# A state-space layer's kernel tables from the distinct bf16 times alone, in a tuned four-layer kernel

## The chip, the cores and the metric

The kernel runs on one core of a Trainium2 chip. Its engines each work through an instruction queue of their own: PE (TensorE: matmuls; PEld is its weight loading), DVE (VectorE), ACT (ScalarE), POOL (GpSimd), and SP (SyncE), whose queue issues most DMAs. An instruction that has to wait for another engine waits at the head of its queue, and everything behind it waits too. The metric is the device time of one execution in microseconds (us), as a median of runs. The order of the instructions on each queue is fixed when the kernel is built.

## The reference

Two kinds of layer, each used twice on `x` of 2048 positions by 512 channels, each with a layer norm ahead of it and a residual behind it. The A layer is a state-space convolution; the B layer is attention over a window of 8 positions, 2 apart, with 32 heads of 16.

```python
l = arange(L).astype(bfloat16)            # L = 2048
P = exp(logdA[:, :, None] * l[None, None, :])     # D = 512, N = 128
K = einsum("dn,dnl,dn->dl", Cc, P, dB).real
y = irfft(rfft(pad(K)) * rfft(pad(u)))[:L] + u * Dskip
...
x = x + A(layernorm(x)); x = x + B(layernorm(x))
x = x + A(layernorm(x)); x = x + B(layernorm(x))
```

The times `l` are rounded to bf16. bf16 keeps 8 bits of a number, so only 641 different times are left of 2048: every one up to 256, then every 2nd, 4th and 8th. The kernel `K` is therefore piecewise constant beyond 256.

## The kernel before

There are five planned parts: preparation, kernel tables with the first convolution, the first B layer (B1), the second A layer (A2, which reuses the spectrum of `K` from DRAM) and the second B layer (B2). "Stage 1" below is the first two parts. In each part, `Plan.op` collects operations; the order in which they are issued is a list of numbers written out in `ORDERS`, one string for each part, and with it each engine's queue is fixed. `pl.either` names two ways for one piece of work (a copy on ACT or on DVE, a transposition by DMA or by PE), and the list takes one.

**Preparation** (`prepare`). From the parameters it forms the pole's step `exp(dt A)`, its repeated squares (the ladder `lad`, L630/L634), and from each of them the multipliers that the tables need, in bf16, in an A and a B form, so that a complex product is two elementwise products and one sum with the halves of the second exchanged (`multipliers`, L579). It normalizes the first input `X` (L196 on DVE, L692 on ACT), and it makes the tables of unit 0 and most of unit 1.

**Tables** (`Tables`). A unit `hc` is 64 channels; there are 8. The kernel at lag `32 i + e` is a product of a power from an X table (`e`, 32 of them) and one from a Y table (64 of them). For each unit, DVE doubles the number of powers level by level: `level` (L406/L411 for the A product, L412 for the B product), `level_sum` (L419) for the sum; `high` and `high_sum` (L426, L427, L432) for the upper half of the X table; `y_product` (L475) for the Y tables. Some of the sums are done by two identity matmuls on PE into PSUM (`sum_mm`, L450 and L451) and an ACT copy back (L455). The tile `Ttab` has two buffers, so the next unit's tables may be built while PE still reads the last one's. Channels lie in pairs (`t`) with real and imaginary part (`c`) and the power (`e`) in the order `h c e t`.

**Contraction** (`contract`, L488 and L491): 256 small matmuls for each unit sum over the 128 states and give K for 64 channels in PSUM (`psk`). It is copied to `KTq`, stored to `k_scratch` in DRAM (L839 is the line of `store`), and fetched from there in the arrangement that the FFT wants (`KT`, L846). The last 64 channels don't take the trip; they go by `spread_rows` and other matmuls (`last`).

**The convolution.** An FFT of length 4096 in two steps. The first (`spectrum`, L862 `ps_s`) multiplies by constant matrices `F1`; ACT copies the result to `Z` (L867), which is transposed by DMA or by PE (`pt`) into `zt`; the second step multiplies by `C2` (`xp`), and ACT copies to `sp_u` or `sp_k`. `u_fft` does that for the input and `k_fft` for `K`, for each group `dc` of 128 channels. DVE then multiplies the spectra (L952, `pa`) and in some places joins the four partial products to two (L957, L958; elsewhere PE does the joining, with more matmuls into `vp`). The inverse gives `vp`, `VT` (L979), `ps_y` (L999) and adds into `X` (L1003). All PSUM results of this part but `psk` share three buffers, `psA`, each of which comes free when ACT or DVE has copied it out. DVE's and ACT's queues are in order, PE's too.

## Time and profile before

| what | us |
|---|---|
| median of 3 runs (lowest, highest) | 467.45 (466.55, 467.87) |
| span of the profiled execution | 468.0 |
| DVE busy, share of the span | 440.1, 94% |
| PE busy | 396.0, 85% |
| ACT busy | 347.7, 74% |
| first work of B1 on DVE (end of stage 1) | 199.56 |
| mean granted clock of TensorE | 0.991 |

The page gives, for each group of instructions, line, engine, operation and tiles, then the count, the busy time in us, the mean duration of one in ns, and the idle time of the engine just before them with what ended it. A duration runs from an instruction's start to its end; back-to-back instructions overlap a little, so the distance from one start to the next is the better price of one. Windows give each engine's busy time, with the number of instructions, in a stretch of the span. In timelines a row is start, duration, instruction, and in square brackets the idle time before it and its releaser.

The 40-slice view shows the shape:

```profile
PE   2520866879799999899999989979999999999996
DVE  6999999999999998699999999989996899999995
ACT  6999857897788898666796357999996667763452
```

Each slice is 11.7 us. The first 17 of them are stage 1.

### The profile page before, as it was taken

What the parts mean: (1) busy time and instruction counts of PE and PEld (TensorE: products, weight loads), DVE (VectorE), ACT (ScalarE), POOL (GpSimd) and SP (SyncE); (2) the same over time, 40 slices, a digit from 0 to 9 for tenths busy, and PEclk for the clock granted to TensorE, in tenths of its full rate; (3) what the DMA queues carried; (4) which work ended last, traced back from release to release, by engine and by line L of the source; (5) the groups of instructions that cost most, each with busy time, mean ns of one, the idle gap of its engine ahead of it and who ended that gap; (6) DMA issues with size and microseconds to landing.
All of it is one profiled execution on the core that took longest, in us unless ns stands there. A gap on an engine that the chain in (4) does not pass through costs nothing. (4 is left out here: it accounts for less than half of the span.)

```text
span 468.0 us, 12380 instructions
## 1 busy us (share of the span) xinstructions
PE 396.0 (85%) x5248; PEld 243.6 (52%) x5248; DVE 440.1 (94%) x595; ACT 347.7 (74%) x543; POOL 21.2 (5%) x90
## 2 busy tenths in 40 slices
PE   2520866879799999899999989979999999999996
PEld 1310543535576667643576444666776445563453
DVE  6999999999999998699999999989996899999995
ACT  6999857897788898666796357999996667763452
POOL 1000000000000001300000000000000010100210
PEclk9999999999999999999999989989999999999999
DMA  8992263047596684640113131389957200213584
GB/s 234 187 287 92 14 148 92 11 83 147 130 205 114 137 173 142 122 69 1 63 46 89 46 67 23 62 254 169 161 107 109 57 22 14 79 46 78 60 157 123
DMA packets 111419, 49.36 MB, mean 105 GB/s; under 512 B 88811, under 2 KB 104572, under 8 KB 111108
## 3 DMA queue, kind: packets, MB, share of 16 engines
q1 hardware_dynamic: 109924, 47.70, 47.5%
q0 software_dynamic: 1152, 0.61, 1.0%
q8 instruction: 41, 0.67, 0.6%
q10 hardware_dynamic: 288, 0.26, 0.2%
q14 instruction: 14, 0.11, 0.1%
HBM read 15.88 MB, written 8.13 MB: 51 GB/s over the span
## 5 line engine op out<-in xcount | busy, mean ns | idle before, releaser
L1755 DVE TENSOR_TENSOR prod<-VX,L 128x512 bf16<-128x512 bf16 (+2 forms) x72 | 75.2, 1101 | 0.7 <-PE po L1771 0.3
L1579 DVE TENSOR_TENSOR prod<-qT,kT 128x4096 bf16<-128x4096 bf16 (+1 forms) x40 | 72.3, 1857 | 1.6 <-ACT qT L1504 1.5
L1771 PE MATMUL po<-prod,sb_ident 128*128 128x512 bf16 x224 | 52.0, 379 | 2.1 <-DVE prod L1755 1.1
L1771 PEld LDWEIGHTS <-sb_ident 128*128 128x128 bf16 x224 | 21.7, 98 | 27.7 <-issue 2.3
L450 PE MATMUL ps_sum<-Ttab,sb_ident 128*128 128x512 bf16 x36 | 14.7, 408 | 22.0 <-DVE Ttab L411 21.2
L1855 PE MATMUL ps_o<-wo_t,oT 128*128 128x512 bf16 x128 | 32.3, 379 | 0.0
L1534 PE MATMUL ps_v<-wv,U 128*128 128x256 bf16 x256 | 31.3, 272 | 1.0 <-ACT L L1718 0.3
L867 ACT CAST Z<-ps_s 128x1024 bf16<-128x1024 f32 (+1 forms) x32 | 29.3, 986 | 2.5 <-PE ps_s L862 1.8
L1480 PE MATMUL ps_qk<-U,wqk 128*128 128x512 bf16 x128 | 29.7, 379 | 0.2 <-ACT qT L1485 0.2
L1545 ACT ACTIVATE VX<-ps_v,rs 128x256 bf16<-128x256 f32 x64 | 26.5, 471 | 4.5 <-PE ps_v L1534 4.1
L1534 PEld LDWEIGHTS <-U 128*128 128x128 bf16 x256 | 24.4, 98 | 8.9 <-issue 4.3
L1499 PE MATMUL ps_qk<-U,wqk 128*128 128x512 bf16 x128 | 29.0, 379 | 0.0
L475 DVE TENSOR_TENSOR Ttab<-Ttab,MPA 128x2048 bf16<-128x2048 bf16 (+2 forms) x20 | 28.4, 1431 | 0.1
L1789 ACT CAST ot<-po 128x1024 bf16<-128x1024 f32 x14 | 13.9, 1013 | 18.2 <-PE po L1771 18.2
L475 DVE TENSOR_TENSOR Y2tab<-Ttab,MPB 128x6144 bf16<-128x6144 bf16 (+1 forms) x13 | 27.2, 2119 | 0.0
L488 PE MATMUL psk<-Ttab 128*32 128x64 bf16 x1024 | 20.7, 197 | 6.1 <-issue 3.2
L488 PEld LDWEIGHTS <-Ttab 128*32 128x32 bf16 x1024 | 18.1, 95 | 10.9 <-issue 9.5
L455 ACT CAST Ttab<-ps_sum 128x1024 bf16<-128x1024 f32 (+1 forms) x22 | 18.2, 873 | 7.0 <-PE ps_sum L451 6.8
L1590 PE MATMUL Lp<-prod,sb_bones 128*32 128x512 bf16 x256 | 21.0, 411 | 1.9 <-DVE prod L1579 1.7
L412 DVE TENSOR_TENSOR Ttab<-Ttab,MUB 128x256 bf16<-128x256 bf16 (+4 forms) x36 | 22.3, 621 | 0.0
L491 PE MATMUL psk<-Y2tab,Ttab 128*32 128x48 bf16 x1024 | 20.3, 190 | 1.9 <-issue 1.3
L952 DVE TENSOR_TENSOR pa<-sp_u,sp_k 128x2048 bf16<-128x2048 bf16 x16 | 19.3, 1220 | 2.2 <-ACT X L1003 1.0
(255 smaller groups left out, 1020.1 us busy)
## 6 DMA issues: line engine op xcount, KB each, us to landing
kt_scratch<-sp_k SPq DMA_DIRECT2D x16, 256.0 KB, 2.9
Kt<-kt_scratch SPq DMA_DIRECT2D x16, 256.0 KB, 5.5
X<-in_A_u_dram SPq DMA_DIRECT2D x8, 256.0 KB, 5.3
X<-in_A_u_dram SPq DMA_DIRECT2D x4, 512.0 KB, 6.0
out_dram<-X SPq DMA_DIRECT2D x16, 128.0 KB, 2.4
k_scratch<-KTq SPq DMA_DIRECT2D x7, 256.0 KB, 2.4
KT<-k_scratch SPq DMA_DIRECT2D x7, 256.0 KB, 3.8
VX<-VX SPq DMA_DIRECT2D x4, 448.0 KB, 3.7
```

What stands on the lines that cost most here:

```text
L412: nc.vector.tensor_tensor(self.spare(hc, False)[:, x0:x1, :, :, 0:m, :].rearrange("n x h c e t -> n (x h c) e t"), src, mult(1), ALU.mult)
L475: nc.vector.tensor_tensor(d, src.to_broadcast([128, c, n, 2 * EYB]), mm, ALU.mult)
L488: nc.tensor.matmul(o.rearrange("e (s i) -> e s i", s=2), xs, T[:, 1:3, h, m // 2, :, t], start=(m == 0), stop=False, skip_group_check=True)
L867: nc.scalar.copy(box["Z", kind, dc][:, 0:n // 8, :, jq * 32:(jq + 1) * 32].rearrange("p g r k -> p r g k"), box.pop(("s1", kind, dc, jq))[ ...
L1480: nc.tensor.matmul(ps[:], wqk[:, ct, f0:f0 + 128], XT[:, ct // 2, 4 * s:4 * s + 4, ct % 2, :], start=(ct == 0), stop=(ct == 3))
L1499: nc.tensor.matmul(box[name][:, k * 512:k * 512 + 512], wqk[:, ct, f0:f0 + 128], XT[:, ct // 2, 4 * s:4 * s + 4, ct % 2, :], start=(ct == ...
L1534: nc.tensor.matmul(ps[:, jj].rearrange("p t h d -> p (t h d)"), XT[:, ct // 2, j + jj, ct % 2, :], wv[:, ct, fp * 256:(fp + 1) * 256], sta ...
L1545: nc.scalar.activation(out, ps, ACT.Identity, scale=r)
L1579: nc.vector.tensor_tensor(pr[:], windows(q, 0, 2), windows(kT[fp][:, a:a + n2, col(w):col(w) + 1024], -DIL * 128, 2), ALU.mult)
L1755: nc.vector.tensor_tensor(p2[:].rearrange("p w j t d h -> p w (j t) d h"), windows(v, -DIL * 256, taps), l.to_broadcast([128, taps, nj * 2 ...
L1771: nc.tensor.matmul(po[:, c:c + 512], ident[:], p2[:, t, k + j:k + j + 2].rearrange("p j t d h -> p (j t d h)"), start=first, stop=stop)
L1855: nc.tensor.matmul(ps, oT[:, ft // 2, o:o + 128], wo_t[:, ft, :], start=(ft == 0 and not res), stop=(ft == 3))
```

## The change

The kernel `K` is built only at the lags that bf16 times can take. Every lag is the sum of one of 20 Y lags and one of 32 X lags (multiples of 8), so a unit has 20 + 32 powers in place of 64 + 32. One tile `Ttab` holds them, in the order `h e c t`, and a second tile `Btab` holds the last product of the X table, whose sum is left out: the contraction takes both terms. Neither has a second buffer: a unit uses the half of the tile given by its parity. The tables are built in chunks of one or two units (`CHUNKS`), the first two within the preparation. Each `step` is a product by the A multiplier, one by the B multiplier into a scratch tile, and an add (`add`) which reads the scratch with real and imaginary part exchanged (`[:, :, ::-1]`). The sums by PE and ACT are gone, and so are the multipliers for one more power and for a cube.

The contraction still has 256 matmuls a unit, with 24 columns. Its result is copied to `kq`, 72 small matmuls with a constant (`select`, `sel`) move the rows to where they are wanted (`pk`), and two copies put them in `KT`; the store to and the fetch from DRAM are gone, and `last` with them. As `K` is piecewise constant, the first FFT step of `K` takes 31 constant pairs of matrices `FK` (2 MB, loaded by four DMAs on GpSimd's queue), by which a row of `KT` stands for all times that share it. Lag 0 is a sum of its own (`k0_sum`), added with `Dskip` as a second row of `D2`.

All five orders in `ORDERS` are new; with them 12 pairs of joins are on DVE where 7 were. Two constants (`minus`, `down`) are loaded after stage 1. The diff, cut to its core (the orders, the multipliers' arrangement, removed functions and renamed arguments are left out; line numbers used for the changed kernel are: seed L424, products L456 and L463, add L468, contraction L481, `D2` L704, `FK` L769, first FFT step L825, products of spectra L916):

```diff
+Y_LAGS = (258, 262, 516, 260, 264, 520, 772, 776, 1032, 1288, 1544, 1800, 1, 5, 2, 6, 3, 7, 4, 8)
+NY, NX, NKC = 20, 32, 24
+X_LAGS = tuple(8 * e for e in range(NX))
+TOP = (1032, 1288, 1544, 1800)
+SLOTS = (TOP + (264, 776, 520, 8), TOP + (516, 772, 260, 4), (1, 5, 2, 6, 258, 3, 262, 7))
...
-    def __init__(self, nc, tc, es, M, cb):
-        self.nc, self.M, self.cb = nc, M, cb
-        self.tt = es.enter_context(tc.tile_pool(name="t_t", bufs=2))
-        self.ty = es.enter_context(tc.tile_pool(name="t_y", bufs=1))
-        self.T, self.Y2 = {}, {}
+    def __init__(self, nc, tc, es, M):
+        self.nc, self.M = nc, M
+        pool = es.enter_context(tc.tile_pool(name="t_t", bufs=1))
+        self.scratch = es.enter_context(tc.tile_pool(name="t_s", bufs=2))
+        self.T = pool.tile([128, UNIT, NY + NX, 2, 2], BF, name="Ttab")
+        self.B = pool.tile([128, UNIT, 32, 2, 2], BF, name="Btab")
+        self.cb1 = pool.tile([128, D // 2, 2, 2], BF, name="cb1")
+        self.box = {}
...
+    def seed(self, copy, u, n):
+        h0, p0 = u % 2 * 32, u * 32
+        copy(self.T[:, h0:h0 + 32 * n, self.Y0].rearrange("n h c t -> n h (c t)"),
+             self.cb1[:, p0:p0 + 32 * n].rearrange("n h c t -> n h (c t)"))
+    def views(self, u, n, what):
+        h0, p0, M = u % 2 * 32, u * 32, self.M
+        T = self.T[:, h0:h0 + 32 * n]
+        ps = slice(p0, p0 + 32 * n)
+        if what in (0, 1, 2):
+            m = 4 << what
+            v = T[:, :, self.Y0:self.X0 + 8].rearrange("n h (x e) c t -> n h x (e c t)", x=2)
+            return v[:, :, :, 0:m], v[:, :, :, m:2 * m], [self.spread(x[:, what, ps].rearrange("p h x c t -> p (h x) c t"), 1 << what) for x in M.joint]
+        if what in (3, 4):
+            m = 4 << what
+            v = T[:, :, self.X0:].rearrange("n h e c t -> n h (e c t)")
+            return v[:, :, 0:m], v[:, :, m:2 * m], [self.spread(x[:, what - 3, ps], 1 << what) for x in M.single]
...
+    def times(self, u, n, what):
+        src, dst, (ma, mb) = self.views(u, n, what)
+        nc.vector.tensor_tensor(dst, src, ma, ALU.mult)
+        if what == 4:
+            h0 = u % 2 * 32
+            b = self.B[:, h0:h0 + 32 * n, 16:].rearrange("n h e c t -> n h (e c t)")
         else:
+            t = self.box[u, what] = self.scratch.tile([128, UNIT * 16], BF, name="Tscr", tag="Tscr")
+            b = t[:, 0:self.elements(n, what)]
+        nc.vector.tensor_tensor(b, src, mb, ALU.mult)
+    def add(self, u, n, what):
+        dst = self.views(u, n, what)[1]
+        b = self.box.pop((u, what))[:, 0:self.elements(n, what)].rearrange("n (e c t) -> n e c t", c=2, t=2)[:, :, ::-1]
+        self.nc.vector.tensor_tensor(dst, dst, b, ALU.add)
-    def level_sum(self, hc, lev, x0=0, x1=2):
-        m = 1 << lev
-        d = self.T[hc][:, x0:x1, :, :, m:2 * m, :].rearrange("n x h c e t -> n (x h) c (e t)")
-        b = self.spare(hc, False)[:, x0:x1, :, ::-1, 0:m, :].rearrange("n x h c e t -> n (x h) c (e t)")
-        self.nc.vector.tensor_tensor(d, d, b, ALU.add)
...
+    def contract(self, psk, u, ds0, ds1):
+        nc, T, B = self.nc, self.T, self.B
         for ds in range(ds0, ds1):
             for m in range(4):
                 for g in range(4):
+                    d = g * 16 + ds
+                    h, t, c = u % 2 * 32 + d // 2, d % 2, m % 2
+                    xs = T[:, h, self.X0:, c, t] if m < 2 else B[:, h, :, 1 - c, t]
+                    y = T[:, h, 0:12, c, t]
+                    rhs = bass.AP(y.tensor, y.offset, [list(y.ap[0]), [32, 2], [4, 12]])
+                    nc.tensor.matmul(psk[32 * g:32 * g + 32, ds, :].rearrange("p (z y) -> p z y", z=2), xs, rhs, start=(m == 0), stop=(m == 3),
+                                     skip_group_check=True)
+CHUNKS = ((0, 1), (1, 1), (2, 2), (4, 2), (6, 1), (7, 1))
+EARLY = 2
+def table_ops(pl, nc, T, u, n, seeds, free, casts):
+    e = T.elements
+    o = moved(pl, nc, ("seed", u), 0.15 + 0.1 * n, 0.08 + 0.066 * n, lambda copy: T.seed(copy, u, n), seeds, free)
+    steps, last = {}, []
+    def step(what, *after):
+        steps[what] = []
+        for v, m in ((u, 1), (u + 1, 1)) if n == 2 and what in (2, 3) else ((u, n),):
+            us, key = e(m, what) / 1920 + 0.069, ("sc", v, what)
+            a = pl.op("V", 2 * us, lambda v=v, m=m: T.times(v, m, what), *after, take=[] if what == 4 else key)
+            if what != 4:
+                a = pl.op("V", us, lambda v=v, m=m: T.add(v, m, what), a, drop=key)
+            steps[what].append(a)
+        return steps[what]
+    def cast(*ks):
+        return [casts[k] for k in ks] if casts else []
+    for lev in range(3):
+        o = step(lev, o, cast(*T.JOINT[lev]))
+    step(3, o, cast(6))
+    a = step("a", o, cast(8))
+    b = step("b", o, cast(9))
+    c = step("c", b, cast(8))
+    d = step("d", c, cast(9))
+    return [step(4, steps[3], cast(7)), a, step("e", d, cast(9))]
...
+    def k0_sum():
+        ps = box["k0"] = pst.tile([1, D], F32, name="k0", tag="ptq")
+        nc.tensor.matmul(ps[:], ones[:, 0:1], cb[:, :, 0, :], start=True, stop=True)
+    a = pl.op("P", 0.25, k0_sum, modes[2], pl.outer(("raw", "block")), take=("ptq", "k0"))
+    moved(pl, nc, ("k0",), 0.48, 0.61, lambda copy: copy(D2[0:1, :], box.pop("k0")[:]), a, drop=("ptq", "k0"))
...
+    def start_sum():
+        o = T.cb1[:].rearrange("n p c t -> n p (c t)")
+        nc.vector.tensor_tensor(o, o, box["cbs"][:, :, ::-1], ALU.add)
...
-        pl = Plan(T=2, Y2=1, psk=2, psA=3, Z=1, zt=4, KT=1, kt=4, xc=8, pa=2, VT=1)
+        pl = Plan(psk=2, kq=2, psA=3, Z=1, zt=4, KT=2, kt=4, xc=NXC, pa=2, VT=1, sc=2)
+        def contract(u):
+            def mm(ds):
+                if ds == 0:
+                    box["psk", u] = psK.tile([128, 16, NKC], F32, name="psk", tag="psk")
+                T.contract(box["psk", u], u, ds, ds + 4)
+            def evac(copy):
+                kq = box["kq", u] = kp.tile([128, NKC, 16], BF, name="kq", tag="kq")
+                copy(kq[:].rearrange("p y d -> p d y"), box.pop(("psk", u))[:])
+            def select():
+                kq = box.pop(("kq", u))
+                pk = box["pk", u] = psK.tile([128, 4, 2, 3, 16], F32, name="pk", tag="psk")
...
+            def placed(copy):
+                if u % 2 == 0:
+                    box["KT", u // 2] = kp.tile([128, 3, 2, 128], BF, name="KT", tag="KT")
+                c0 = u % 2 * UNIT
+                pk = box.pop(("pk", u))
+                for e in range(2):
+                    copy(box["KT", u // 2][:, :, e, c0:c0 + UNIT].rearrange("p s (g d) -> p g s d", g=4), pk[:, :, e])
+            p = []
+            for ds in range(0, 16, 4):
+                p = [pl.op("P", 0.54, lambda ds=ds: mm(ds), Td[u], p, take=[] if ds else ("psk", "k", u))]
+            Cd[u] = p
+            a = moved(pl, nc, ("psk", u), 0.4, 0.48, evac, p, take=("kq", u), drop=("psk", "k", u))
+            a = pl.op("P", 0.6, select, a, take=("psk", "sel", u), drop=("kq", u))
+            Kd[u] = moved(pl, nc, ("placed", u), 0.5, 0.55, placed, a, [] if u % 2 == 0 else Kd[u - 1], take=[] if u % 2 else ("KT", u // 2), drop=("psk", "sel", u))
...
+        def k_fft(dc, b0, nb):
+            c0, c1 = b0 * 32, (b0 + nb) * 32
+            def mats(j, r):
+                x = box.get(("KT", dc))
+                todo = [(FK[:, i, r, :], x and x[:, s // 2, s % 2, c0:c1]) for s, i in pairs[j]]
+                if j == 0 and r == 0:
+                    todo.append((C["onesr"][:], D2[:, dc * DCH + c0:dc * DCH + c1]))
+                return todo
+            last = [("KT", dc)] if b0 + nb == 4 else []
+            spectrum("k", dc, b0, nb, mats, lambda jq: [Rd["FK", jq], *[Kd[u] for u in range(dc * 2, dc * 2 + 2) if (u % 2) * 2 < b0 + nb]], last)
+            for c in range(b0, b0 + nb):
                 keep(dc, c)
         def keep(dc, c):
...
-        for hc in range(1, 8):
-            dc = hc // 2
-            tables(hc)
-            contract(hc - 1)
-            store(hc - 1)
-            if hc % 2 == 0:
-                u_fft(dc)
-                k_fft(dc - 1)
-            else:
-                if dc:
-                    for c in range(4):
-                        inverse(dc - 1, c, product(dc - 1, c))
-                    final(dc - 1, 8)
-        k_fft(3)
-        contract(7)
-        for n in range(2):
-            last(n)
-        for c in range(4):
-            inverse(3, c, product(3, c))
-        final(3, 4)
+        for u in range(8):
+            for u0, n in CHUNKS[EARLY:]:
+                if u0 == u:
+                    o = table_ops(pl, nc, T, u0, n, [], [Cd[x - 2] for x in range(u0, u0 + n)], None)
+                    for x in range(u0, u0 + n):
+                        Td[x] = o
+            contract(u)
+            dc = u // 2
+            if dc == 3:
+                k_fft(3, u % 2 * 2, 2)
+            elif u % 2:
+                k_fft(dc, 0, 4)
+            if u % 2:
+                if dc < 3:
+                    u_fft(dc + 1)
+                for c in range(4):
+                    inverse(dc, c, product(dc, c))
+                final(dc, 4 if dc == 3 else 8)
```

At the start of the first convolution the new orders give PE and DVE these queues (x counts instructions, seed and add are DVE's):

```
PE:  first step of u, dc 0: 4 groups of 8 (L825); transposes pt x32 (L855);
     first step of u, dc 1: 1 group; contraction of unit 0, x128; 1 group; contraction of unit 0, x128;
     2 groups; second step xp of u, dc 0, 1 group; contraction of unit 1, x256; xp, 2 groups; selection of unit 0; ...
DVE: ... products L456 and L463 of unit 1; copy of D2 from k0 (L704); seed of units 2 and 3 (L424); products and adds of units 2 and 3; ...
```

In the built program, the first L825 on PE waits for the copy of `D2` (the pool of `psA` opens in the place of the preparation's PSUM tiles), and the seed L424 waits for the last matmul of unit 1's contraction, the last reader of `Ttab`.

More of the change, by code (lines that the diff above doesn't have):

```diff
@@ L615, in prepare @@
     now, cur = [modes[0], modes[1]], lambda: LAM
-    for i in range(11):
+    for i in range(10):
         drop = [("lad", i)] if i else []
         sqs = []
-        if i < 10:
+        if i < 9:
             def square(cur=cur, i=i):
@@ L696, in prepare @@
     pl.op("S", TAIL, lambda: None, xn)
-    seeds = [pl.op("G", 0.4, lambda: T.ones(0))]
-    seeds.append(moved(pl, nc, ("seed", 0), 0.2, 0.15, lambda copy: T.seed(copy, 0), seeds, modes[2], modes[3]))
-    o, sums = {0: [seeds], 1: [seeds]}, []
-    for lev in range(4):
-        for x in (1, 0):
-            us = vt(128 << lev) if lev else 0.25
-            a = vec(2 * us, lambda lev=lev, x=x: T.level(0, lev, x, x + 1), o[x], casts[lev if x else lev + 6])
-            o[x] = vec(us, lambda lev=lev, x=x: T.level_sum(0, lev, x, x + 1), a)
-            sums.append(o[x])
@@ L906, in by_pe @@
                     return pl.op("A", 0.92, turn_evac, a, drop=key)
-                t = pl.either(("turn", kind, dc, i), by_dma, by_pe) if both else by_dma()
+                t = pl.either(("turn", kind, dc, i), by_dma, by_pe)
                 key = ("psA", "s2", kind, dc, i)
@@ L1952 @@
     more, VX = b_weights(nc, const2, B_wo)
+    for name, arr, dt in (("minus", _bf(-np.eye(128)), BF), ("down", np.eye(128, k=1, dtype=np.float32), F32)):
+        C[name] = load_const(nc, const2, name, arr, dt)
     Wt.update(more)
```

491 lines of the change are left out of this document (151 added, 340 removed), and 118 rows, old and new, of the table ORDERS.

## The prediction

> **What bounds the kernel now.** I read the busy line first, then the engines in three windows (start of the tables, rest of the first stage, everything later), the columns being PE, PEld, DVE, ACT, POOL, clock, DMA share and GB/s, and last the timelines.
>
> ```profile
> PE 396.0 (85%) x5248; PEld 243.6 (52%) x5248; DVE 440.1 (94%) x595; ACT 347.7 (74%) x543; POOL 21.2 (5%) x90
> 0.00:48.00 48.00, 12.32 (x338) 9.20 (x339) 44.03 (x88) 42.83 (x70) 2.26 (x13) 1.00 0.78 195
> 48.00:199.50 151.50, 130.74 (x3025) 89.24 (x3025) 143.60 (x156) 120.06 (x150) 7.47 (x13) 1.00 0.57 117
> 199.50:468.00 268.50, 252.99 (x1886) 145.19 (x1885) 252.50 (x352) 184.84 (x324) 11.43 (x64) 0.98 0.40 83
> ```
>
> The reader is to see that up to 199.5 us (kernel tables and first convolution, "stage 1") DVE is full while PE starts the stage idle, and that afterwards DVE and PE are equally full, 94% each. So DVE work taken out of stage 1 can shorten it; the 268.5 us behind it are another matter. The stage's DVE time is tables:
>
> ```profile
> L475 DVE TENSOR_TENSOR Ttab<-Ttab,MPA 128x2048 bf16<-128x2048 bf16 (+2 forms) x20 | 28.4, 1431 | 0.1
> L475 DVE TENSOR_TENSOR Y2tab<-Ttab,MPB 128x6144 bf16<-128x6144 bf16 (+1 forms) x13 | 27.2, 2119 | 0.0
> L412 DVE TENSOR_TENSOR Ttab<-Ttab,MUB 128x256 bf16<-128x256 bf16 (+4 forms) x36 | 22.3, 621 | 0.0
> L450 PE MATMUL ps_sum<-Ttab,sb_ident 128*128 128x512 bf16 x36 | 14.7, 408 | 22.0 <-DVE Ttab L411 21.2
> L455 ACT CAST Ttab<-ps_sum 128x1024 bf16<-128x1024 f32 (+1 forms) x22 | 18.2, 873 | 7.0 <-PE ps_sum L451 6.8
> ```
>
> Instructions overlap at their ends, so I price one by the distance to the next start (columns: start, duration, instruction):
>
> ```profile
> 42.48 0.69 DVE L412 TENSOR_TENSOR Ttab<-Ttab,MUB 128x1024 bf16<-128x1024 bf16 x1
> 43.08 0.42 DVE L419 TENSOR_TENSOR Ttab<-Ttab 128x512 bf16<-128x512 bf16 x1
> 43.42 0.41 DVE L196 TENSOR_SCALAR X<-X,ln_rstd_a,ln_nb_a 128x512 bf16<-128x512 bf16 x1
> ...
> 145.64 0.41 DVE L406 TENSOR_TENSOR Ttab<-Ttab,MU 128x256 bf16<-128x256 bf16 x1 [0.46 <-issue]
> 145.94 0.38 DVE L412 TENSOR_TENSOR Ttab<-Ttab,MUB 128x256 bf16<-128x256 bf16 x1
> 146.24 1.22 DVE L426 TENSOR_TENSOR Ttab<-Ttab,MHA 128x2048 bf16<-128x2048 bf16 x1
> 147.37 1.22 DVE L427 TENSOR_TENSOR Ttab<-Ttab,MHB 128x2048 bf16<-128x2048 bf16 x1
> ...
> 199.56 1.08 DVE L1419 BATCH_NORM_STATS2 pst<-X 128x6 f32<-128x256 bf16 x3 [2.87 <-PE ps_y L999]
> ```
>
> 1024 elements cost 0.60 us, 512 cost 0.34, 2048 cost 1.135: n/1920 + 0.068. The level-0 operations at 145.6 cost 0.30 for 256 elements where this line gives 0.20: their operands are single 4-byte words standing apart. The last row is the stage's end: DVE's first work of the next layer, 199.6 us.
>
> **The tables, from 129 to 84.5 us of DVE.** Before, a unit of 64 channels has 24,064 elements of products (levels 7,680, L426/L427 4,096, L475 12,288). Eight units: 192,512/1920 = 100.3, with 121 instructions of 0.068 (8.2), level 0's surplus (2.8), and 33 sums on DVE (28,400 elements, 17.0): 128.3, say 129; the other sums run on PE and ACT. After, steps 0 to 4 and a to e hold 6,400 elements a unit, formed twice, and 4,352 are added: 17,152 a unit, 137,200/1920 = 71.5, plus 186 instructions x 0.068 = 12.6, 84 in all. Everything else on DVE in stage 1 nets +5.6: joins of products 14 to 24 instructions (+3.3 by 0.335), the starting pole 3 x 0.60, more copies and norms (VT, X, D2, KT, kq: +4.7), less one ladder power, the cube and one weight product (-4.2). DVE in stage 1 goes from 184.3 to 145.6: -38.7.
>
> **The unknown price: an add whose second operand has the two words of each 8-byte pair exchanged** (L468; 34,816 elements, and 1,024 in the pole's add). No row shows that. Lower end: streaming, as the 0.34 sum above, whose swapped blocks are 8 bytes or longer. Upper end: level 0's factor, (0.30-0.068)/(0.20-0.068) = 1.75, hence 18.7 x 0.75 = +14 us. It is nearer the sum, since all three operands stay dense in memory and only order changes: I take 0.
>
> [...]
>
> **PE and ACT.** PE loses the sums (72 x 0.2135 = 15.4) and 40 inverse matmuls of 512 (4.3); it gains first-stage matmuls by constant rows (443 for 326, +6.5), 576 selections at the contraction's 8.5 ns (4.9, less 1.8 for the old spreading), the rest +4: 126.5 to 120.6. ACT loses L455 and falls from 157 to 130. Neither is the bound by sum. The 14 scratch DMAs (256 KB, 2.4 and 3.8 us to landing) no longer lie between contraction and FFT; DVE never waited for them: 0 on the path. The 2 MB of constant rows come by GpSimd's queue, four loads; at the 6.0 us of the page's 512 KB loads that is 24 us one after the other. They wait for the transposed input's last reader, around 45 us, and are wanted after 70: hidden, 6 us (one load) if not. GpSimd's queue has only memsets behind them. SP loses 14 issues; the two constants moved to the end of the stage are first used in the softmax, far later: 0.
>
> **The new wait.** Before, `Ttab` had two buffers; now one, in halves by unit parity. In the changed order DVE's seed of units 2 and 3 (L424) waits for PE's last contraction of unit 1. That stands on PE behind the whole u-FFT of dc 0 up to its transposes and the four first-stage groups of dc 1. And the first of those matmuls waits for DVE's copy of `D2` (L704), the last operation of the preparation, because the new PSUM pool takes its bank. So PE begins when DVE ends. Prices:
>
> ```profile
> 50.90 3.46 PE L862 MATMUL ps_s<-X,sb_F 128*128 128x128 bf16 x32
> 52.69 3.73 ACT L867 CAST Z<-ps_s 128x1024 bf16<-128x1024 f32 x4
> ```
>
> DVE's work to that point is 47.7 us; with the 5.1 us that DVE stood still in the same preparation before, t0 = 52.8. Then: first eight matmuls of a PE just out of idle (0.108 each) and their latency 1.2; ACT's four evacuations of `Z` at 0.93, to 4.9; gap to the first transposed block 1.1; four more at 0.93 to 9.75, gap 0.45, two `Z` to 12.1; one second-stage group 1.0; 256 contractions x 8.5 ns = 2.2: **15.4 us** of DVE idle. Queued behind the seed stand all tables of units 2 and 3, and their contraction and k-FFT wait for those. Later handovers have their contraction earlier in the order; there DVE's 20 us per pair of units faces about 20 of ACT, and I allow 2.6 us. The tail: before, DVE stood still 7.3 us from 160 us to 199.6; the chain behind the last tables is as before, plus selection for spreading: 7.3 again.
>
> **Sum.** Stage 1 ends at 145.6 + 5.1 + 15.4 + 2.6 + 7.3 = 176.0, against 184.3 + 5.1 + 2.9 + 7.3 = 199.6: -23.6. In the later layers the instructions are nearly the same (DVE 244.8 to 247.5, PE 236.2 to 234.6 us by these prices) in a new order: 0, within 3 either way. 468.0 - 23.6 = **444.4 us**; the profiled execution is 0.55 above the median, so 444.
>
> **Rivals.**
> (a) *Slow adds.* Word exchange at level 0's price: +14, of which some 2 lie under waits for ACT: 456. For it: 145.6's row; against: the operand is dense. [...]
> (b) *No stall.* If DVE's hand-over costs nothing (u-FFT ahead of the preparation's end), 444.4 - 15.4 = 429. Against: the order written down.
> (c) *Slower: the single buffer makes ACT the bound at every handover.* Units 4-5, 6 and 7 each seed after a contraction that stands behind FFT groups sharing three PSUM buffers which ACT alone empties, 12 evacuations x 0.93 = 11.2 us each: 3 x 11.2 - 2.6 = +31, 475. It decides from +23.6, that is from 8.7 us a handover. For it: ACT and DVE equal per pair of units; against: ACT falls by 27 us over the stage and L455's turn in the same buffers goes.
> (d) *The smaller tables don't show*, since later layers take longer by what stage 1 wins (their 94% DVE and PE leave no slack, new orders could cost): 467.
>
> **Chances.** Forecast 0.46, (a) 0.25, (b) 0.12, (c) 0.13, (d) 0.04. The forecast's own range is 439 to 450 (orders 3, handovers 3). With (a) and half of (b), and a part of what lies between (a) and (c), 429 to 464 holds 8 in 10. Under 0.3% (1.4 us) this measurement can't tell from no change: faster 0.83, same 0.03, slower 0.14.
>
> **What would show it.** DVE idle some 15 us near 53 us with PE's contraction of unit 1 as releaser (else the wait is wrong); L468 at 512 elements starting 0.335 after its predecessor (0.5 would be (a)); DVE's first statistics of the next layer near 176; 268 us behind it. Several gaps of 9 us or more at the seeds L424 would be (c), and the forecast is wrong if stage 1 ends after 190 with L468 at full rate.

## The result, and the profile after

The changed kernel takes 505.94 us (median; 505.26 to 507.46) against 467.66 us for the kernel before in the same comparison: a ratio of 1.0817, 95% interval 1.0789 to 1.0845. It is slower by 38 us where 24 us less was forecast, and outside the predicted range. Its profiled execution spans 504.3 us, so the sum that gave 444.4 us is short by 59.9 us.

First the busy line of the changed kernel, then three rows of its 40-slice view (a slice is 12.6 us), then its engines in three windows: to the end of the preparation, the rest of stage 1, everything later (columns as in the prediction).

```profile
PE 399.8 (79%) x5751; PEld 242.6 (48%) x5751; DVE 413.8 (82%) x673; ACT 329.3 (65%) x513; POOL 26.4 (5%) x82
...
PE   1610458948937796889899979987999999999895
...
DVE  7999408936948673869999998998898789999995
...
PEclk9999998967977898999999997999999999999999
```

```profile
0.00:55.00 55.00, 11.66 (x337) 9.08 (x337) 51.40 (x114) 38.05 (x63) 7.72 (x16) 1.00 0.72 195
55.00:225.96 170.96, 130.23 (x3607) 95.66 (x3608) 104.45 (x184) 107.42 (x125) 6.06 (x1) 0.88 0.41 82
225.96:504.30 278.34, 257.94 (x1807) 137.84 (x1806) 257.98 (x377) 183.78 (x326) 12.61 (x65) 0.99 0.38 81
```

DVE's total did fall, from 440.1 to 413.8 us busy, and all of the fall is in stage 1: 51.4 + 104.5 = 155.9 us where it was 187.6; behind stage 1 it rose by 5.5. But stage 1 became longer, 225.96 us where it was 199.56. In the second window nobody is full: PE 130 of 171 us, DVE 104, ACT 107, and PE's granted clock is 0.88 on average. The 40 slices show the holes: between slices 4 and 12 PE and DVE are low together three times, so neither of them fills the time.

The long waits of DVE in stage 1, from its timeline (in square brackets the idle time before the row and what ended it):

```profile
77.60 0.23 DVE L424 COPY Ttab<-cb 128x256 bf16<-128x256 bf16 x1 [21.90 <-PE psk L481]
...
112.75 0.23 DVE L424 COPY Ttab<-cb 128x256 bf16<-128x256 bf16 x1 [8.50 <-PE psk L481]
...
123.86 1.23 DVE L916 TENSOR_TENSOR pa<-sp_u,sp_k 128x2048 bf16<-128x2048 bf16 x1 [3.83 <-ACT sp_k L851]
...
148.25 0.20 DVE L424 COPY Ttab<-cb 128x128 bf16<-128x128 bf16 x1 [6.38 <-PE psk L481]
...
167.67 1.23 DVE L916 TENSOR_TENSOR pa<-sp_u,sp_k 128x2048 bf16<-128x2048 bf16 x1 [5.64 <-ACT sp_k L851]
...
200.53 1.77 DVE L780 CAST kq<-psk 128x384 bf16<-128x384 f32 x1 [7.60 <-PE psk L481]
...
225.96 0.75 DVE L1317 BATCH_NORM_STATS2 pst<-X 128x6 f32<-128x256 bf16 x2 [3.65 <-PE ps_y L963]
```

Four times DVE waits for `psk`, the contraction, and twice for the spectrum of `K`, which is computed from it. All idle times of over 0.15 us in stage 1 add up to 68.5 us, so DVE's work there, priced from start to start, is 225.96 - 68.5 = 157.5 us. Set against the prediction's terms:

| term of the sum | predicted | measured | difference |
|---|---|---|---|
| DVE's work in stage 1 | 145.6 | 157.5 | +11.9 |
| wait at the first seed | 15.4 | 21.9 | +6.5 |
| later handovers: 8.50, 6.38, 7.60 at `psk`, 3.83 and 5.64 at `sp_k` | 2.6 | 32.0 | +29.4 |
| remaining idle time (preparation, tail) | 12.4 | 14.6 | +2.2 |
| the layers behind stage 1 | 268.5 | 278.3 | +9.8 |

That is the 59.9 us, to rounding. The groups of the changed kernel say what the contraction itself was doing (columns: busy time, mean ns, then the idle time of the engine before them and what ended it):

```profile
L481 PE MATMUL psk<-Ttab,Btab 128*32 128x24 bf16 x1024 | 20.5, 184 | 17.2 <-issue 17.2
...
L780 ACT CAST kq<-psk 128x384 bf16<-128x384 f32 x7 | 12.6, 1867 | 28.5 <-PE psk L481 28.5
...
L481 PE MATMUL psk<-Ttab 128*32 128x24 bf16 x1024 | 20.5, 184 | 10.3 <-issue 9.8
...
L481 PEld LDWEIGHTS <-Btab 128*32 128x32 bf16 x1024 | 18.8, 114 | 17.8 <-issue 17.8
```

PE stood idle in front of contraction instructions, and what ended the wait is "issue": no other engine, no DMA of data, nothing that the profile shows as a semaphore. The view of line 481 alone sums it up as 29 waits:

```profile
its engine sat idle before it (us, times) until:
  issue: 58.0, 29
```

(This view adds the weight loads' waits to the matmuls', and most of them are the same time counted twice; the matmuls alone waited 17.2 + 9.8 = 27.0 us.) Four windows, each from one such restart of PE to the next, and DMA in a stretch with the second pair, in slices of 0.35 us:

```profile
103.79:107.79 4.00, 1.25 (x128) 1.14 (x129) 0.46 (x1) 0.00 (x0) 0.00 (x0) 0.52 0.17 61
107.79:111.52 3.73, 1.25 (x129) 1.15 (x129) 0.00 (x0) 0.00 (x0) 0.00 (x0) 0.50 0.02 4
143.93:147.93 4.00, 1.25 (x128) 1.15 (x128) 0.00 (x0) 0.00 (x0) 0.00 (x0) 0.62 0.02 5
147.93:151.66 3.73, 1.26 (x128) 1.16 (x128) 3.27 (x10) 1.89 (x1) 0.00 (x0) 0.50 0.02 4
```

```profile
GB/s 23 23 23 0 0 47 0 0 0 0 0 0 0 0 0 0 0 47 0 0 0 0 0 0 0 0 0 47 0 0 0 0 0 0 0 0 0 0 47 0
...
q8 instruction: 4, 0.07, 2.3%
```

The numbers fit each other. Between two restarts there are 128 matmuls and as many weight loads (to within one), 256 instructions, in 1.25 us of work and 3.73 to 4.00 us of time. In the 14 us from 143 us the DMA rate shows four lone peaks of 47 GB/s for 0.35 us, 16 KB each, about 3.5 to 4.2 us apart, and the queue named "instruction" moved four packets. Over the whole program that queue has 45 packets for 2 x 5751 PE instructions, and 41 for 2 x 5248 before: one packet for 256 instructions each time. Counting PE's instructions through the trace makes it sharper. In stage 1, after the preparation, fifteen of PE's stops, 0.4 to 4.6 us each and 32.2 us in all, lie whole multiples of 256 instructions apart: the first six follow each other after 256, 256, 512, 512 and 256. In the last three of the four windows the DMA engines are 2% busy, so other traffic doesn't explain the distance between the packets.

So in these dense runs of small matmuls PE works off 256 instructions in 1.25 us, and the next 256 start 3.73 to 4.00 us after them: 3.73/128 = 29 ns for a matmul and its load, where starts within a block lie about 8.5 ns apart. That PE waits there for the next packet of instructions is read from these numbers; no view names that wait. This was the theory that the experiments had to try.

### The profile page after: what moved, and what is told of

It reads as the page before. It is cut to its first block, busy times and chain, and to the rows that moved or that the text cites. A ratio compares the mean times of both kernels' runs of the same rounds, so it can differ in the third digit from the quotient of the medians.

```text
span 504.3 us, 13346 instructions
## 1 busy us (share of the span) xinstructions
PE 399.8 (79%) x5751; PEld 242.6 (48%) x5751; DVE 413.8 (82%) x673; ACT 329.3 (65%) x513; POOL 26.4 (5%) x82
## 4 chain that ended last, share of the span: by engine, by line
PE 44%; DVE 32%; issue 11%; ACT 10%; DMA 2%; ACTq 0%; DVEq 0%; SPq 0%
DVE prod L1477 6%; DVE prod L1653 6%; PE psk L481 4%; PE ps_qk L1378 4%; PE ps_s L825 4%; PE ps_o L1753 3%; PE ps_qk L1397 3%; PE po L1669 3%; DVE Ttab L456 2%; PE Lp L1488 2%; DVE pst L1317 2%; DVE Ttab L468 2%; PE ps_y L963 1%; DVE Tscr L463 1%; PE vp L1156 1%
## 5 line engine op out<-in xcount | busy, mean ns | idle before, releaser
L1669 PE MATMUL po<-prod,sb_ident 128*128 128x512 bf16 x248 | 58.9, 379 | 2.7 <-DVE prod L1653 2.4
L828 ACT CAST Z<-ps_s 128x1024 bf16<-128x1024 f32 (+1 forms) x36 | 31.5, 942 | 18.8 <-PE ps_s L825 18.5
L825 PE MATMUL ps_s<-X,sb_F 128*128 128x128 bf16 x128 | 12.2, 265 | 31.7 <-DVE D L704 29.2
L481 PE MATMUL psk<-Ttab,Btab 128*32 128x24 bf16 x1024 | 20.5, 184 | 17.2 <-issue 17.2
L780 ACT CAST kq<-psk 128x384 bf16<-128x384 f32 x7 | 12.6, 1867 | 28.5 <-PE psk L481 28.5
L1687 ACT CAST ot<-po 128x1024 bf16<-128x1024 f32 (+1 forms) x17 | 15.6, 935 | 23.4 <-PE po L1669 23.4
L424 DVE COPY Ttab<-cb 128x256 bf16<-128x256 bf16 (+1 forms) x3 | 0.7, 220 | 36.8 <-PE psk L481 36.8
L916 DVE TENSOR_TENSOR pa<-sp_u,sp_k 128x2048 bf16<-128x2048 bf16 x16 | 19.3, 1221 | 12.8 <-ACT sp_k L851 10.7
L481 PE MATMUL psk<-Ttab 128*32 128x24 bf16 x1024 | 20.5, 184 | 10.3 <-issue 9.8
L481 PEld LDWEIGHTS <-Btab 128*32 128x32 bf16 x1024 | 18.8, 114 | 17.8 <-issue 17.8
L456 DVE TENSOR_TENSOR Ttab<-Ttab,MSA 128x256 bf16<-128x256 bf16 (+4 forms) x44 | 26.1, 592 | 0.2
L468 DVE TENSOR_TENSOR Ttab<-Ttab,Tscr 128x256 bf16<-128x256 bf16 (+2 forms) x58 | 25.7, 469 | 0.5
```

Source lines behind the costliest of these rows:

```text
L456: nc.vector.tensor_tensor(dst, src, ma, ALU.mult)
L468: self.nc.vector.tensor_tensor(dst, dst, b, ALU.add)
L481: nc.tensor.matmul(psk[32 * g:32 * g + 32, ds, :].rearrange("p (z y) -> p z y", z=2), xs, rhs, start=(m == 0), stop=(m == 3), skip_group_c ...
L825: nc.tensor.matmul(ps[:, r, 0:n // 8, jj * 8:(jj + 1) * 8], w, x, start=(k == 0), stop=(k == len(todo) - 1))
L1669: nc.tensor.matmul(po[:, c:c + 512], ident[:], p2[:, t, k + j:k + j + 2].rearrange("p j t d h -> p (j t d h)"), start=first, stop=stop)
```

## The experiments

The theory, A: the contraction is supplied with instructions too slowly, and since `Ttab` has one buffer the delay falls on DVE at each handover; beside it stand smaller terms, namely the early wait, the copy of `kq` and the order of the later layers. Its rivals: the single buffer and the copies alone make the handovers long, through ACT and the PSUM buffers, and the "issue" time only lies beside them; or the new orders are to blame. The numbers of each stand in the expectations. The differences in us below are between medians and the changed kernel's 505.94; the ratios are to the kernel before, run beside each (467.66 to 468.19 us). Some diffs are shortened.

**The copy of `kq` written in line.** The changed kernel's copy writes 384 elements of 2 bytes 32 bytes apart; the edit turns the loops, so that it writes in line and reads PSUM apart.

```diff
-copy(kq[:].rearrange("p y d -> p d y"), box.pop(("psk", u))[:])
+copy(kq[:], box.pop(("psk", u))[:].rearrange("p d y -> p y d"))
```

> One line of the changed kernel: the copy of psk to kq (L780) loops over the lag first, so that it writes 2-byte elements one behind the other and reads PSUM in strides, as the kernel before did in its copy of 512 elements (0.59 us); the changed kernel reads in line and writes in strides of 32 bytes, 1.82 us for 384. The copy should fall to about 0.5 us, 8 x 1.3 = 10.6 us less on ACT and DVE. Theory A (the handovers of the single-buffered table are set by PE, whose instructions arrive one block of 256 in 3.7 to 4.0 us): DVE's stalls before the seeds stay within 1 us each, the total gains 1.5 to 5 us. Theory B (ACT, which empties the shared PSUM buffers, sets them): the total gains 8 to 11 us.

Measured: 501.73 us, ratio 1.0726 (1.0676 to 1.0776), 4.2 us less than the changed kernel. The form view of the copy (min, median and max ns):

```profile
L780 ACT CAST kq<-psk x7: 478/479/513, 72.6 to 170.6; 128x384 bf16<-128x384 f32 x7
```

A copy of 1.82 us became 0.48, and eight of them gave about 4 us: a real term, not the cause. The waits at the seeds were still 21.8, 8.0 and 5.8 us.

**The later layers in the order of before.** B1, A2 and B2 get the old lists of `ORDERS`; the first two parts keep the new ones.

```diff
-ORDERS = [new preparation, new first convolution, new B1, new A2, new B2]
+ORDERS = [new preparation, new first convolution, old B1, old A2, old B2]
```

> The changed kernel with the three orders of the later layers (B1, A2, B2) as they were before; stage 1 is untouched. Later layers took 268.5 us before and 278.3 after. If the new orders cost these 9.8 us: 496 us in all, B1 back from 114.3 to about 107.7 and B2 from 102.2 to about 97.7. If they are longer because of what stage 1 leaves behind (constants loaded later, where tiles lie, the clock): no change, 506.

Measured: 493.12 us, ratio 1.053 (1.0484 to 1.0576), 12.8 us less. In the profile the layers behind stage 1 take 268.8 us instead of 278.3, as before the change; stage 1, which this edit doesn't touch, came out 3.4 us shorter, so some us of such a comparison can be variation from execution to execution. The new orders of the later layers cost 9.5 us, and the rival of the orders holds for that share. Which places in them cost it wasn't tried, and the order of stage 1 isn't tested by this.

**Half of the contraction.** Only the terms from `Ttab` are summed; those from `Btab` are left out, so K is not the reference's.

```diff
-            for m in range(4):
+            for m in range(2):
...
-start=(m == 0), stop=(m == 3)
+start=(m == 0), stop=(m == 1)
```

> The changed kernel with half of its contraction: the two of four matmuls that take Btab are left out, so a unit has 128 matmuls and as many weight loads, one block of 256 instructions in place of two. K is then not the reference's. Theory A (instruction supply): the idle time named issue before L481 falls from about 58 us (both halves and weight loads together) to under half, DVE's stalls before the seeds from 21.9, 8.5 and 6.4 to about 17, 2 and 2; stage 1 loses 15 to 20 us. Theory B (PE's own time or ACT): half of the matmuls is 1024 x 8.5 ns = 8.7 us of PE in all, at most 4 of it where DVE waits.

Measured: 474.14 us, ratio 1.0129 (1.0074 to 1.0184), 31.8 us less. The direction is theory A's, but the size is well above the 15 to 20 us that were expected under it. Counted by blocks, afterwards, half of 16 blocks is saved: 8 x 3.73 = 30. At 8.5 ns the same 1024 matmuls would be worth 8.7. The view of line 481 and DVE's seeds in this kernel:

```profile
  issue: 10.7, 11
```

```profile
69.58 0.23 DVE L424 COPY Ttab<-cb 128x256 bf16<-128x256 bf16 x1 [13.88 <-PE psk L481]
...
97.60 0.23 DVE L424 COPY Ttab<-cb 128x256 bf16<-128x256 bf16 x1 [0.79 <-PE psk L481]
...
125.50 0.19 DVE L424 COPY Ttab<-cb 128x128 bf16<-128x128 bf16 x1
...
192.55 7.61 DVE L1317 BATCH_NORM_STATS2 pst<-X 128x6 f32<-128x256 bf16 x23 [3.65 <-PE ps_y L963]
```

With the same buffers, copies and orders, the second and third handover cost 0.8 us and nothing, and stage 1 ends at 192.6. The rival that the single buffer and the copies alone make the handovers long falls: with them unchanged, the handovers are short as soon as PE's contraction is.

**PE free to begin earlier.** The copy of `D2` is issued in the middle of the preparation instead of as its last operation.

```diff
-"... 264 244 180 117 109 188 112 119 265 120 166 ... 280 218 208 232 236",
+"... 264 244 180 117 109 188 112 119 265 236 120 166 ... 280 218 208 232",
```

> The changed kernel with DVE's copy to D2 (L704) issued in the middle of the preparation, not as its last operation; nothing else. If that copy holds back PE, PE's first matmul of the convolution (L825) moves from 55.9 us to about 44, where ACT's last norm of X ends, and DVE's first stall falls from 21.9 us to 8 to 10, as the contraction of units 0 and 1 still waits for their tables: total -12, 494 us. If the stall belongs to the supply of instructions alone, PE starts early and the seed still comes 18 us or more after the tables: total within 4 us of 506.

Measured: 495.26 us, ratio 1.0575 (1.053 to 1.062), 10.7 us less. In this kernel (its line numbers are lower by 52) PE starts 13.7 us earlier, and the first seed comes 9.8 us earlier:

```profile
42.14 2.72 PE L773 MATMUL ps_s<-X,sb_F 128*128 128x128 bf16 x24 [15.31 <-DVE X L236]
```

```profile
67.78 0.23 DVE L372 COPY Ttab<-cb 128x256 bf16<-128x256 bf16 x1 [12.19 <-PE psk L429]
...
103.43 0.23 DVE L372 COPY Ttab<-cb 128x256 bf16<-128x256 bf16 x1 [8.74 <-PE psk L429]
```

The hand-over that the prediction had read in the queues is there, and without it 10.7 of the expected 12 us come back. The first wait fell to 12.2 us and not to the expected 8 to 10, and the second handover is as long as it was.

**The same number of matmuls, narrower.** Three of four have 12 columns instead of 24; the other 12 columns of their terms are left out.

```diff
-psk[32 * g:32 * g + 32, ds, :], xs, rhs
+psk[32 * g:32 * g + 32, ds, 0:12 if m else 24], xs, rhs if m == 0 else y
```

> The changed kernel with as many contraction matmuls and weight loads, but three of four take 12 columns in place of 24 (60 columns in place of 96 for each channel); the terms of 8 Y lags are left incomplete, so K is not the reference's. Theory A (the count of instructions): no change, 503 to 507 us, L481's idle time named issue stays near 58 us. Theory B (the array's time in the contraction): up to 37% of the contraction's 17 us, 500 us, and the idle time falls.

Measured: 504.54 us, ratio 1.079 (1.0767 to 1.0812); "issue" in front of line 481 still 51.1 us in 27 waits. That is 1.4 us less, within the 503 to 507 that theory A gave. Columns are not what costs here; with the halved contraction above (31.8 us less), it is the count of instructions.

**The last step's sum on DVE.** This computes the full K with half of the matmuls: DVE adds the scratch to the X table in place, `Btab` shrinks to a scratch of 16 powers, and GpSimd's filling of its zeros goes.

```diff
+        if what == 4:
+            nc.vector.tensor_tensor(dst, dst, self.B[:, h0:h0 + 32 * n].rearrange("n h e c t -> n (h e) c t")[:, :, ::-1], ALU.add)
...
-            for m in range(4):
+            for m in range(2):
...
-                    xs = T[:, h, self.X0:, c, t] if m < 2 else B[:, h, :, 1 - c, t]
+                    xs = T[:, h, self.X0:, c, t]
```

> The changed kernel, correct in full, with the last step's sum done by DVE as in the other steps (add of 2048 elements a unit, 8 x 1.135 = 9.1 us more on DVE), so that the contraction takes two matmuls a channel in place of four. Theory A (instruction supply): half the contraction was worth 31.8 us, so -32 + 9 = 483 us; the seeds' stalls as without that half (13.9, 0.8, none). Theory B (PE's own time or the buffers): the same 9 us of DVE lie on the path and little comes back, 508 to 512.

Measured: 478.17 us, ratio 1.0225 (1.019 to 1.0259), 27.8 us less, though DVE does six more adds (four of 2048 elements at 1.22 us, two of 4096 at 2.29). Stage 1 ends at 196.6, the "issue" time is 10.0 us and the first seed waits 13.89 us, as in the halved contraction. (Line numbers are higher by 2 in this kernel and the next ones with the sum.) One thing comes on top of the sum here: without GpSimd's filling DVE starts its work some 3 us earlier, as the last experiment shows. So of the 27.8 us up to 3 may belong to that, and the runs don't separate them.

**All four corrections together** (`kq` in line, `D2` early, later layers in the old order, the sum on DVE), and for comparison the three without the sum. The edits are those shown above:

```diff
+copy(kq[:], box.pop(("psk", u))[:].rearrange("p d y -> p y d"))
+"... 119 265 236 120 166 ..."
+ORDERS = [new preparation with 236 moved, new first convolution, old B1, old A2, old B2]
+nc.vector.tensor_tensor(dst, dst, <B with its halves exchanged>, ALU.add)
```

> The three edits that helped one by one (kq written in line -4.2, later orders of before -12.8, early copy to D2 -10.7) and the sum on DVE with half the contraction (-23 expected): if they add up, 455 us, faster than before's 467.5. If the stalls they remove are partly the same ones (the early start and the shorter contraction both take from the first stall, 12.2 and 13.9 us left of 21.9), 460 to 466.

> The three edits without the sum on DVE: the contraction keeps its 256 matmuls a unit. If they add up: 506 - 4.2 - 12.8 - 10.7 = 478 us, still slower than before, so that under theory A what is left of the loss is the supply of PE's instructions: gaps of 2 to 3 us named issue inside L481, DVE's stalls before the second and third seeds still 8 and 5 us. If the supply doesn't matter once PE starts early: below 470.

Measured: 456.51 us with all four, ratio 0.9757 (0.9739 to 0.9775); 482.25 us with three, ratio 1.031 (1.0295 to 1.0326). The seeds of the kernel with all four, and what is left of the waits in its stage 1:

```profile
58.46 0.23 DVE L424 COPY Ttab<-cb 128x256 bf16<-128x256 bf16 x1 [2.10 <-PE psk L483]
...
87.58 0.23 DVE L424 COPY Ttab<-cb 128x256 bf16<-128x256 bf16 x1 [1.00 <-PE psk L483]
...
136.53 1.23 DVE L918 TENSOR_TENSOR pa<-sp_u,sp_k 128x2048 bf16<-128x2048 bf16 x1 [3.36 <-ACT sp_k L853]
...
187.92 1.08 DVE L1319 BATCH_NORM_STATS2 pst<-X 128x6 f32<-128x256 bf16 x3 [3.65 <-PE ps_y L965]
```

So the change does pay, 11 us, once the contraction has half the instructions and the other three corrections are in. The edit of the sum decides between slower and faster: it is worth 25.7 us on top of the other three (GpSimd's filling, which goes with it, included). Without it the second and third seeds still wait 8.18 and 5.40 us, the 8 and 5 that theory A expected. Singly the four gave 4.2 + 12.8 + 10.7 + 27.8 = 55.5 us; together 49.4.

**The tail.** On top of the four, the last two blocks of `K`'s spectrum are transposed by PE instead of by DMA.

```diff
-"... 589 ... 599 ... 594 ..."
+"... 589 600 601 595 596 ..."
```

> The kernel of e7_all with the last two blocks of K's spectrum turned by PE and ACT (two groups of 8 transposes, two copies of 0.93 us) and not by DMA, where PE waited 2.6 us for the second step's input and DVE then 3.7 us for sp_k, 10 us ahead of the stage's end. If that wait sets the end: -3 to -4 us, 453 us. If the three shared PSUM buffers or ACT take it back: 456 to 457, no change.

Measured: 454.85 us, ratio 0.9717 (0.9683 to 0.9752), 1.7 us less than with the four. That is about half of what was expected, and the two intervals overlap, so the gain itself is not settled. Both versions beat the kernel before and the changed one; this has the lowest median.

**The kernel before with half of its contraction.** It leaves out the products with `Y2tab`.

```diff
-            for m in range(4):
+            for m in (0, 2):
```

> The kernel before with half of its contraction: the matmuls that take Y2tab are left out, so K is not the reference's; it keeps 128 matmuls a unit, as e3_half does in the changed kernel (-31.8 us). Theory A as refined (the supply of instructions costs time only where DVE has to wait for the contraction; with Ttab in two buffers it doesn't): 0 to -3 us, 465 to 468. If dense contraction costs every kernel alike: -15 us or more.

Measured: 467.04 us, ratio 0.9971 (0.9948 to 0.9994), 1 us or so less than the kernel before beside it. So before the change the contraction's count cost next to nothing, although its rows carried the same sign:

```profile
L488 PE MATMUL psk<-Ttab 128*32 128x64 bf16 x1024 | 20.7, 197 | 6.1 <-issue 3.2
...
L488 PEld LDWEIGHTS <-Ttab 128*32 128x32 bf16 x1024 | 18.1, 95 | 10.9 <-issue 9.5
```

The sign was weaker, too. The views of its two lines, L488 and L491, give

```profile
  issue: 12.7, 18
...
  issue: 3.4, 3
```

together 16.1 us where the changed kernel has 58.0. Of stops at the same multiples of 256 instructions there are six in stage 1, 6.2 us, where the changed kernel has fifteen and 32.2. PE's timelines suggest why: before, the contraction's matmuls come in 20 pieces of 32 to 192, with other matmuls in between; in the changed kernel up to 512 follow each other without a break. So two things can have kept the contraction off DVE's path before: the second buffer, and these pieces. The runs don't separate them, and an order of stage 1 with the contraction in pieces wasn't tried in the changed kernel.

**`Btab`'s zeros by DVE.** In the changed kernel GpSimd fills them at the start; here DVE does it as its first instruction, while it has nothing else.

```diff
-        nc.gpsimd.memset(self.B[:, :, 0:16], 0.0)
+                nc.vector.memset(T.B[:, :, 0:16], 0.0); raw = load_params(nc, pp, prm)
```

> The changed kernel with the zeros of Btab's first half written by DVE as its first instruction, not by GpSimd. In the changed kernel DVE's first small operation (128x4) lasted 3.22 us, to the same moment as GpSimd's memset (2.86 + 3.55 us), where it lasted 0.17 before. If GpSimd's memset holds DVE back, it lasts 0.17 again and the preparation ends up to 3 us earlier; DVE's own memset lies in the 3.2 us in which it waits for its first input. In all -1 to -3 us; if the 3.22 us belong to a load that is late, no change.

Measured: 505.82 us (500.26 to 506.29), ratio 1.0768 (1.0716 to 1.0821): no difference in the total that can be told. The profile does show the effect at its place. In the changed kernel the first DVE instruction and GpSimd's memset end together at 6.4 us; with the zeros by DVE the same instruction takes 0.17 us:

```profile
3.21 3.22 DVE L549 TENSOR_SCALAR dtw<-dtb 128x4 f32<-128x4 bf16 x1 [3.21 <-ACT dtb L547]
```

```profile
2.86 3.55 POOL L414 MEMSET Btab<- 128x4096 bf16 x1
```

```profile
1.25 1.76 DVE L735 MEMSET Btab<- 128x2048 uint32 x1 [1.25 <-PEq L1915]
3.22 0.17 DVE L549 TENSOR_SCALAR dtw<-dtb 128x4 f32<-128x4 bf16 x1 [0.20 <-ACT dtb L547]
```

Stage 1 ended 3.0 us earlier in that execution, but its whole span was 504.5 us. That the 3 us are worth something in the total stays open.

A second buffer for `Ttab` in the changed kernel wasn't tried, so what it alone would give back isn't shown.

## Why the prediction was wrong, step by step

**The step that failed** is the price "256 contractions x 8.5 ns = 2.2", and with it "Later handovers have their contraction earlier in the order; ... I allow 2.6 us". The 8.5 ns are the distance of two starts within a burst. A unit's contraction is 512 PE instructions, two blocks, and takes about 2 x 3.73 = 7.5 us when nothing longer stands between its matmuls (each pair of windows above shows two blocks in 4.00 + 3.73 us). In the kernel before, the burst was a fair price: DVE had a second buffer and no long wait there names the contraction, and halving it was worth 1 us. The change took that buffer away, which the prediction saw, and so put PE's real rate on DVE's path, which it didn't. The runs show that this rate is what cost: half the count -31.8 and -27.8 us, half the columns in three of four 1.4. That the loss of the buffer made it cost is an argument from the waits at the seeds; the long runs that the new order of stage 1 makes may have their share, 512 matmuls where the old had at most 192.

The sign was on the page of before: "10.9 <-issue 9.5" for the weight loads. Here idle time with "issue" as its releaser, before a run of many small instructions, was in good part a rate limit (six stops at multiples of 256 instructions, 6.2 us), though one that cost next to nothing yet. In the changed kernel 256 instructions, as many as one 16 KB packet of the instruction queue stands for, follow the 256 before them only after 3.73 to 4.00 us in the windows above, and their work is 1.25.

**The first wait** was right in mechanism (the releaser is PE's contraction, and PE had waited for the copy of `D2`) and too small, 15.4 for 21.9. With the contraction halved it is 13.9, where the prediction's terms give 14.3 (15.4 less half of 2.2), so the rest of that term (first stage, four evacuations of `Z`, transposes) was priced about right. The 8 us between 21.9 and 13.9 are about two blocks at 3.73. Two slips in the working changed nothing: the terms of the 15.4 add up to 15.3, and the inverse matmuls that it calls "of 512" have 256 columns, which is what their 4.3 us stand for. PE's first group shows the cause of its late start:

```profile
55.85 3.57 PE L825 MATMUL ps_s<-X,sb_F 128*128 128x128 bf16 x32 [29.24 <-DVE D L704]
```

**The tables.** Their price was right in kind: 157.5 us of DVE work against 188.8 by the same counting before, a saving of 31.3 for a predicted 38.7. Of the missing 7.4 us, 3.05 are the start of DVE beside GpSimd's memset, and the one `kq` copy on DVE took 1.77 us instead of about 0.5. The rest is a price that I had left out: a table instruction that reads the result of the one just before starts about 0.12 us later. The trace has 28 such places in the tables of stage 1, 3.4 us in all. (The other 4.5 of the table's +11.9 are the kernel before, whose 184.3 counts as 188.8 when priced from its own gaps.)

**The exchanged add at full rate** was right, and rival (a) falls. Four rows of the changed kernel's DVE timeline:

```profile
79.73 0.68 DVE L463 TENSOR_TENSOR Tscr<-Ttab,MJB 128x1024 bf16<-128x1024 bf16 x1
80.45 0.69 DVE L468 TENSOR_TENSOR Ttab<-Ttab,Tscr 128x1024 bf16<-128x1024 bf16 x1
81.18 0.69 DVE L456 TENSOR_TENSOR Ttab<-Ttab,MJA 128x1024 bf16<-128x1024 bf16 x1
...
83.59 1.29 DVE L468 TENSOR_TENSOR Ttab<-Ttab,Tscr 128x1024 bf16<-128x1024 bf16 x2
```

The add of 1024 elements takes 0.69 us, like the product ahead of it, and at 83.59 two of them, the first of which reads an earlier product than the last, take 1.29. So the second starts 0.60 us after the first, as the products do (82.39 and 82.99 in the same timeline); at the factor 1.75 that rival (a) took from level 0 it would be 1.0, by the prediction's line. Here too is the late start: 80.45 is 0.72 after the product it reads, where products follow each other after 0.60.

**Rival (c)** had the shape, several waits at the seeds and a slower kernel, and the wrong agent. It blamed ACT's evacuations; the releaser at the seeds is PE's `psk`, and with the contraction halved ACT's buffers, unchanged, held nobody up at the second and third seed. Its 475 was also far below 505.9.

**Selections, DRAM trip, FK load**: no long wait of DVE in stage 1 names any of them. **The later layers** were taken as 0 within 3 and cost 9.8, and the old lists give 9.5 back. "Nearly the same instructions" doesn't hold for DVE: with the new lists it has 377 instructions there, 258.0 us busy, and with the old ones 352 and 252.6. DVE's added 5.4 us of work are over half of the 9.5 us; whether all of it lies on the path, and which place in the lists costs the rest, wasn't tried.

**The clock** was taken as slow for the first eight matmuls only. In the starved stretches above it is granted at 0.50 to 0.62, and the group behind one of them runs at about half the speed of a group after a busy stretch (the first row):

```profile
90.81 1.05 PE L825 MATMUL ps_s<-KT,FK 128*128 128x128 bf16 x16 [0.24 <-ACT Z L828]
...
115.52 1.78 PE L825 MATMUL ps_s<-X,sb_F 128*128 128x128 bf16 x15 [1.76 <-issue]
```

That is 1.78 us for 15 matmuls of 128 columns, at a granted clock of 0.50, against 1.05 us for 16 at 1.00. What this adds apart from the starving itself wasn't separated.

## What to carry to other kernels

Price a run of many small instructions by its count over a long stretch, not by the distance of two starts in a burst, and read "issue" as a releaser there as a possible rate limit (here 29 ns for a matmul and its load, against 8.5), which a second buffer or other work in between may be hiding. When a change removes such a buffer, ask what the producer's real rate is, since that is now on the path. Moving work between engines can be worth it even towards the busier one: six adds on DVE, some 9 us, took 1024 matmuls and their weight loads from PE's queue, and that edit gave back 26 to 28 us, of which up to 3 may come from GpSimd's filling.

## What the runs showed of the hardware

- The DMA queue named "instruction" moved packets of 16 KB, one for 256 PE instructions (45 for 2 x 5751, 41 for 2 x 5248). In dense small matmuls 256 instructions took 3.73 to 4.00 us, of which 1.25 was work.
- A copy from PSUM that writes 2-byte elements 32 bytes apart took 1.82 us for 384 elements on ACT and 1.77 on DVE; reading PSUM apart and writing in line took 0.48 and 0.56.
- In the changed kernel, while GpSimd filled 128x4096 bf16 with zeros (3.55 us), a DVE instruction on 128x4 elements lasted to the same moment, 3.22 us; with the zeros by DVE it took 0.17.
- A DVE add whose second operand exchanges the two words of each 8-byte pair ran at the rate of a dense product (0.60 us from start to start for 1024 elements); an instruction that reads the result of the one just before started about 0.12 us later (0.72).
